# Row maxima of two banks in turn, layer norm's root on ScalarE, named PSUM banks and a new job order

## The chip, the cores and the metric

The kernel runs on one core of a Trainium2 chip. The metric is device time in microseconds (us); lower is better. TensorE (PE in the profile) multiplies and transposes, VectorE (DVE), ScalarE (ACT) and GpSimd (POOL) do the rest, SyncE (SP) issues most transfers.

## The reference

Two branches read the same layer-normed input and are added to it: an infini-attention (segment-wise softmax attention with a compressive memory) and a mixer MLP.

```python
def _A_ref(x, wq, wk, wv, wo, beta):      # S = 2048, D = 512, H = 32 heads of Dh = 16, N = 4 segments of L = 512
    q, k, v = ...                         # x @ wq, x @ wk, x @ wv, split into heads and segments
    phi = lambda t: jnp.where(t > 0, t + 1.0, jnp.exp(t))
    g = _sigmoid(beta).reshape(1, H, 1, 1)
    for s in range(N):
        qs, ks, vs = q[:, :, s], k[:, :, s], v[:, :, s]
        logits = jnp.einsum("bhqd,bhkd->bhqk", qs, ks) * scale + mask      # causal within the segment
        a_dot = jnp.einsum("bhqk,bhkd->bhqd", _softmax(logits), vs)
        pq = phi(qs)
        a_mem = jnp.einsum("bhld,bhde->bhle", pq, M) / (jnp.einsum("bhld,bhd->bhl", pq, z)[..., None] + 1e-6)
        outs.append(g * a_mem + (1.0 - g) * a_dot)
        M = M + jnp.einsum("bhld,bhle->bhde", phi(ks), vs)
        z = z + jnp.einsum("bhld->bhd", phi(ks))
    return ... @ wo
def _B_ref(x, w1, b1, w2, b2):            # F = 1792
    h = _gelu(_layernorm(x) @ w1 + b1)
    return h @ w2 + b2
xn = _layernorm(x)
return x + _A_ref(xn, ...) + _B_ref(xn, ...)
```

## The kernel before

Everything is cut into jobs, and the program is one list of jobs. `ORDER` is a string with one letter a job; each letter names a stream (keys, queries, row maxima, scores, and so on), and the next job of that stream is written out. Each engine runs its own instructions in the order in which the jobs stand in the list, so `ORDER` fixes every engine's queue and the queues of transfers on SP and POOL. The pools around it put in the waits.

The work in words: `X` jobs load four or two tiles of 128 tokens, take their mean and variance (`norm_stats`), scale them (`norm_apply`) and transpose them on TensorE into `xnT`; `Y` does the same for the MLP branch, with statistics that `norm_stats` has made with the first (a norm of a normed row needs only a second root, so `a` and `y` have two columns a tile). `T` projects the queries or keys of 8 heads of one segment (12 matmuls of 512 columns), splits the result into a high and a low half (`hl`) and sends it through DRAM into the layout `qst`/`kst`. There are 16 steps i (4 segments x 4 groups of 8 heads).

In each step the row maxima come first. `m_jobs(i)` makes 12 jobs, for four pairs of heads t and three sets of query blocks: block 3 alone (512 columns of keys), blocks 2 and 0 together (384 + 128), block 1 (256). A job takes two PSUM tiles, one for each head of the pair, multiplies into both, and VectorE then adds the causal mask and takes the maximum, one instruction and one read-out of its result into `mc` for each block. `R` (`m_row`) transposes `mc` on TensorE, halves it (`mhl`, ACT then DVE) and sends it back as two more rows of the queries. `S` jobs compute the scores transposed, with the maximum already taken off, and ScalarE takes the exponential out of PSUM (`pt`); `pv`/`PV` multiply with the values; `O` divides; `Qd`/`Q`/`K`/`Z`/`N` serve the memory (`ame`, `rc`, `mst`, `zr`, `pkn`). `D` is the MLP's first matmul (`hT`), `G` its gelu, `H` the split into halves on POOL and ACT, `e` the second matmul into two tiles that stay open over 14 jobs, and the sum into `acc` (L761) frees them. `out` is the output projection. `warm` jobs are matmuls on ones that keep TensorE busy at the start.

All PSUM tiles come from one pool of 8 (`dense`), each a bank of 128 x 512 numbers. A job that needs a tile waits, on TensorE, until the bank's last reader is done. ScalarE holds one set of function tables at a time: `plan()` puts a load before the first job that needs exponential and logarithm ("E") after a gelu ("G").

Of the kernel before, what the change touches and what calls it, by code (L numbers as in the profile page):

```python
# [57 lines left out]
def streams():  # L58
# [43 lines left out]


ORDER = (
    "aeatcctutcuettcctcvvvatuaatuacevcaaabcvvbccwtvucwvfbtdvbtwvtvxtxxvyxwxxgwxcxyxxhtoooxywocwoosyyniyyzoiyccziigps"
    "iiznipizyinyzcfzAnsiqpiqAizoqqzizAowvpAoimhoAzizjqpjojqqjcczijqibojiBqikkkAAkjiojiqjmjiqjiqjbsqiikkkpkibbaAfopo"
    "jjlgpojlqjjlaohjAokpkkkajojiqijqjAiqijmiqjiqiAsABiBfpoiqqppikkiqiqkkhilBgpoaapolsjqqqjjqqjjoojiiklkkkijpaiaBoos"
    "jqaqjqqiqjiqqiaaBqijqbqqbijqiqsBiifompkkkkibbplmghpooBojqjojljmlqojqqijqikpkkkpiiojiqjqbjqjiqiqijojqiikkkpkliif"
    "nlnigplnrmjjrjjqjniiriqpijqiqikkkkmhjjjrjipiojqiqijpqikikkkbmilolfsoojmjgjolojqjjobbmkkkkmqjiqjqijqjiqjioijoiqi"
    "pisskkkkaphiiqplpqqimislfaolipoqmogaoosmasqqjqjqqjqqjaqjoiiqqiqqppjiqiqooiiipmkkpkkipioijajoqajajqqqqjjiqqsiaho"  # L110
    "akkkkqjslqlbmbjjfojqqljmgjqbbmkkkkmqjqjjohojiiojiojpiikkkkliinoipilmifnilimnigpmrrjjjnrjijrjiikmbpkkkjspiiooisq"
    "ijqjqijqjqbjmipqqiiiqkkkkhilfoqqqpjlmjgojqjqqpjjlmoookkmkkipjipooisqijqiqjjqiqijqqijbbsikkkppkiqqlaiiqmslhfoiqa"
    "qqmppgpoaooojjqaaomojqjjqiqlsqijqqpiqiikkkkmiasiqqjmiqjqqjjpoahojiaqiqjikpkiaoopiaoobfkkpjbjqqjslqlqqqjmjgobbjq"
    "lkmkkkmqjqqjqjqjiqmjqiooijikkkpkpiiiflplonoiliinmiipgniomnrrpjjjoojibqjqijqqiiqpikkkkiqipjrjjqirspjqjisqiqijpqi"
    "kkkkiolfmooljmjgqjbjojqjlmokkkmkjqpojsiiosbqjisqiqijqjqiqijqikkkpkliifbsqqqliiqqmoipgopmloojjojqqjjoojiikkpkkii"
    "qjqijqijqmjpiiqjsqjiqikipikkkpqqioqploplojjqojqjqjqjolkkkkjjqoqjjqpqjsqjoqqkkkkpqqplqpmqpqqqqqqqpqqqqmlqqqqqqlr"
    "rrr"
)


def plan():

    todo = [iter(st) for st in streams()]
    tab = "E"
    for c in "".join(ORDER):
        key = next(todo[NAMES.index(c)])
        k = key[0]
        need = "G" if k == "G" else "E" if k in ("S", "Q") or k == "O" and key[2] == 0 or k == "T" and (
            key[1] >= NG if key[2] == 0 else key[1] < NU - NG) else tab
        yield key, None if need == tab else need  # L130
        tab = need
# [3 lines left out]
def infini_mixer_kernel(ctx: ExitStack, tc: tile.TileContext, x, wq, wk, wv, wo, beta, w1, b1, w2, b2, out):  # L135
    nc = tc.nc
    V, A, G, T, Q = nc.vector, nc.scalar, nc.gpsimd, nc.tensor, nc.sync
# [171 lines left out]
    def qk_scale(g0, n):  # L309
        p = dense()  # L310
        T.matmul(p[:, :2 * n], ones, am[:, :2 * NG].rearrange("p (w g) -> p w g", w=2)[:, :, g0:g0 + n], start=True, stop=True)
# [55 lines left out]
    FV, SV, FO, SO, CO = range(5)  # L367
    F1, S1, F2, S2, CG, SHH, C2, B1F = range(5, 21, 2)

    I_MAGIC = 0x5F3759DF  # L370

    stats = cst.tile([P, S // P, 2, 2], F32, name="stats")

    def norm_stats(tok, tiles):


        n = len(tiles)
        ag = sm.tile([P, 4, 2], F32, name="ag", bufs=1)[:, :n]
# [16 lines left out]
        V.scalar_tensor_tensor(y, b, 1.875, y, op0=OP.add, op1=OP.mult)
# [16 lines left out]
    def ln(kind, n, b, part):  # L412

        tok = 4 * n + 2 * b if kind == "X" else 2 * n
        if part == 0:
            lt[kind, n, b] = ts = []
            for j in range(2):
                name = ("nN", "nD")[j] if (kind, n, b) == ("X", 0, 1) else "xt"
                t = sb.tile([P, D], F32, name=name, bufs=2 if name == "xt" else 1)
                Q.dma_start(t, x[P * (tok + j):P * (tok + j) + P, :])  # L420
                ts.append(t)
        elif part == 1:
            norm_stats(tok, lt[kind, n, b] + (lt[kind, 0, 1] if n == 0 else []))
        else:
            norm_apply(tok, lt[kind, n, b], kind == "Y", (kind, n, b) == ("X", 0, 1))
# [11 lines left out]
    def ln_tr(t, dst, c0):  # L437
        p = dense()
        for k in range(KT):
            T.transpose(p[:, P * k:P * k + P], t[:, P * k:P * k + P], ident)  # L440
# [128 lines left out]
    def m_jobs(i):  # L569
        def f(t, qbs):  # L570
            def go():
                if i not in mc:
                    mc[i] = sm.tile([P, GH, 4], F32, name="mc", bufs=1)
                ps = dense(), dense()
                o = 0
                for qb in qbs:
                    n = P * (qb + 1)
                    for b, p in enumerate(ps):
                        r = slice(64 * b, 64 * b + KM)
                        T.matmul(p[:, o:o + n], stk[i, 0][r, t, P * qb:P * qb + P], stk[i, 1][r, t, :n],  # L580
                                 start=True, stop=True)
                    o += n
                for b, p in enumerate(ps):
                    o = 0
                    for qb in qbs:
                        n = P * (qb + 1)
                        V.tensor_tensor_reduce(p[:, o:o + n], p[:, o:o + n], mask[:, 512 - n:], 1.0, -3e38,  # L587
                                               OP.add, OP.max, mc[i][:, 4 * b + t, qb:qb + 1])
# [249 lines left out]
    for key, load in plan():  # L838
        if load == "E":
            A.preload_act_table_set("natural_log_exp_and_others")  # L840
        CALL[key[0]](*key[1:])
# [28 lines left out]
```

## Time and profile before

| what | us |
|---|---|
| median of 3 runs | 745.69 (745.43 to 746.32) |
| the profiled execution, whole | 747.66 |
| its span, first to last instruction | 745.9 |
| TensorE busy in it | 708.0 |
| VectorE busy | 562.7 |
| ScalarE busy | 536.1 |
| GpSimd busy | 365.3 |
| mean granted TensorE clock | 0.99 of full |

In the profile's rows a group reads: line, engine, operation, output <- inputs, shape, count, then busy time and the mean of one in ns, then the engine's idle time before them and what ended it. A row of waits reads: who waited, for whom, the sum in us, how often, and the longest. A row in order of time reads: start, duration, what. Row maxima appear as CUSTOM_DVE_ANT_0, followed by DVE_READ_ACCUMULATOR2_ANT, the read-out.

### The profile page before, as it was taken

The page shows a single profiled execution, that of the slowest core. Times are in us where ns is not written, and L with a number is a line of the kernel's source. Part 1 is how long each engine was busy: PE and PEld are TensorE (multiplying, and loading weights), DVE is VectorE, ACT ScalarE, POOL GpSimd, SP SyncE. Part 2 cuts the span into 40 slices and gives each one's busy share as a digit, 9 for nine tenths or more (in the row PEclk, how much of TensorE's full clock was granted, in tenths as well). Part 3 has the DMA queues.
Part 4 walks back from the last instruction along what each step waited for, and adds up shares of the span by engine and source line. Part 5 has one row for each costly group of instructions (what it writes and reads, how often), then busy time and mean ns, then how long its engine had stood idle before and what let it go on. Part 6 is the DMA issues. An engine that isn't in the chain of part 4 may idle for free.

```text
span 745.9 us, 16734 instructions
## 1 busy us (share of the span) xinstructions
PE 708.0 (95%) x6261; PEld 397.7 (53%) x6261; DVE 562.7 (75%) x1721; ACT 536.1 (72%) x920; POOL 365.3 (49%) x548
## 2 busy tenths in 40 slices
PE   7899998999999999899999999989999999999997
PEld 5464655464654455455453556565654545564543
DVE  6789878978884877978688677989478575969233
ACT  5788898775986568576884687767685668767960
POOL 5375657465524344535433446455534255355652
PEclk9699999999999999999999999999999999999999
DMA  9765323132304023240412313340311313330001
GB/s 278 217 200 152 105 54 91 45 101 61 100 2 114 29 81 80 58 114 4 108 23 65 102 47 90 79 109 15 88 44 47 112 16 87 86 102 2 3 16 57
DMA packets 54093, 59.30 MB, mean 79 GB/s; under 512 B 5038, under 2 KB 40892, under 8 KB 54012
## 3 DMA queue, kind: packets, MB, share of 16 engines
q1 hardware_dynamic: 51708, 54.04, 25.3%
q0 software_dynamic: 2304, 4.20, 3.5%
q8 instruction: 49, 0.80, 0.5%
q14 instruction: 32, 0.26, 0.1%
HBM read 41.18 MB, written 17.04 MB: 78 GB/s over the span
## 4 chain that ended last, share of the span: by engine, by line
PE 47%; DVE 32%; ACT 7%; issue 5%; POOL 5%; DMA 2%; POOLq 0%; DVEq 0%; SPq 0%; ACTq 0%
PE dense L455 20%; DVE dense L587 13%; PE dense L754 7%; PE dense L649 6%; PE dense L773 4%; PE dense L620 3%; PE dense L580 3%; DVE mc L587 3%; ACT pt L625 2%; DVE hl L475 2%; PE dense L786 1%; PE dense L440 1%; DVE oT L502 1%; DVE zr L517 1%; DVE phk L484 1%
## 5 line engine op out<-in xcount | busy, mean ns | idle before, releaser
L587 DVE CUSTOM_DVE_ANT_0 dense<-dense,mask 128x512 f32<-128x512 f32 (+3 forms) x512 | 240.6, 516 | 25.1 <-PE dense L580 18.2
L625 ACT ACTIVATE pt<-dense,qkcs 128x512 f32<-128x512 f32 (+1 forms) x384 | 207.6, 623 | 43.0 <-PE dense L620 38.1
L754 PE MATMUL dense<-w2s,hT 64*128 64x512 f16 x1344 | 177.3, 376 | 0.6 <-POOL hT L730 0.2
L455 PE MATMUL dense<-yT,w1s 128*128 128x256 f16 x1344 | 160.6, 273 | 6.3 <-DVE mhl L598 1.8
L634 POOL TENSOR_SCALAR_AFFINE_SELECT pt<-pt 128x256 f32<-128x256 f32 x256 | 103.4, 437 | 103.7 <-ACT pt L625 102.4
L455 PEld LDWEIGHTS <-w1s 128*128 128x128 f16 x1344 | 128.2, 98 | 39.2 <-issue 18.8
L730 POOL TENSOR_TENSOR hT<-hh,hT 128x512 f16<-128x512 f32 x64 | 66.7, 1043 | 89.1 <-ACT hT L729 88.6
L754 PEld LDWEIGHTS <-hT 64*128 64x128 f16 x1344 | 71.0, 94 | 62.0 <-issue 12.8
L649 PE MATMUL dense<-pt,vt 128*32 128x512 f32 (+3 forms) x1024 | 77.9, 436 | 0.6 <-POOL pt L634 0.3
L580 PE MATMUL dense<-kst,qst 48*128 48x128 f16 (+3 forms) x512 | 72.3, 297 | 6.4 <-DVE mc L587 2.7
L620 PE MATMUL dense<-qst,kst 50*128 50x512 f16 (+3 forms) x512 | 72.4, 298 | 5.2 <-DVE mc L587 1.6
L587 DVE DVE_READ_ACCUMULATOR2_ANT mc<- 128x1 f32 x512 | 72.1, 141 | 0.2
L729 ACT ACTIVATE hT<-hh 128x512 f16<-128x512 f32 x64 | 36.8, 575 | 29.4 <-POOL hh L728 29.1
L728 POOL TENSOR_SCALAR hh<-hT,sc 128x512 f32<-128x512 f32 x64 | 42.4, 662 | 31.1 <-ACT hT L721 29.0
L649 PEld LDWEIGHTS dense<-pt,vt 128*32 128x32 f32 x1024 | 32.1, 109 | 42.2 <-issue 32.3
L714 ACT ACTIVATE hT<-dense,b1t,sc 128x256 f32<-128x256 f32 x64 | 36.1, 566 | 19.5 <-PE dense L455 18.7
L620 PEld LDWEIGHTS <-kst 50*128 50x128 f16 x512 | 27.3, 94 | 38.7 <-issue 23.8
L580 PEld LDWEIGHTS <-qst 48*128 48x128 f16 x512 | 28.3, 94 | 35.7 <-issue 21.4
L455 PE MATMUL dense<-xnT,wqs 128*128 128x512 f16 x192 | 46.6, 395 | 0.1
L455 PE MATMUL dense<-xnT,wks 128*128 128x512 f16 x192 | 46.6, 395 | 0.1
L679 POOL TENSOR_TENSOR nN<-nN,oT 128x512 f32<-128x512 f32 x16 | 20.3, 1269 | 50.4 <-DVE oT L503 50.4
L475 DVE SCALAR_TENSOR_TENSOR hl<-dense,hl 128x512 f16<-128x512 f32 x32 | 22.1, 690 | 29.9 <-ACT phq L474 11.9
(222 smaller groups left out, 1022.5 us busy)
## 6 DMA issues: line engine op xcount, KB each, us to landing
xt<-in_A_x_dram SPq DMA_DIRECT2D x30, 256.0 KB
kd<-hl SPq DMA_DIRECT2D x48, 128.0 KB
kst<-kd SPq DMA_DIRECT2D x32, 192.0 KB
qd<-hl SPq DMA_DIRECT2D x48, 128.0 KB
qst<-qd SPq DMA_DIRECT2D x32, 192.0 KB
acc<-in_A_x_dram SPq DMA_DIRECT2D x16, 256.0 KB
acc<-in_B_b_dram POOLq DMA_DIRECT2D x16, 256.0 KB, 4.3
out_dram<-acc SPq DMA_DIRECT2D x16, 256.0 KB
```

The source lines that it names most:

```text
L455: T.matmul(p, wsl(ws, k, a), xsl(xs, k, b), start=s0 and i == 0, stop=s1 and i == 3 * n - 1)
L475: V.scalar_tensor_tensor(hl[:, 1, :], p, float(2 ** -16), hl[:, 0, :], op0=OP.mult, op1=OP.subtract)
L580: T.matmul(p[:, o:o + n], stk[i, 0][r, t, P * qb:P * qb + P], stk[i, 1][r, t, :n], start=True, stop=True)
L587: V.tensor_tensor_reduce(p[:, o:o + n], p[:, o:o + n], mask[:, 512 - n:], 1.0, -3e38, OP.add, OP.max, mc[i][:, 4 * b + t, qb:qb + 1])
L620: T.matmul(p[:, o:o + n], stk[i, 1][r, t, P * kb:P * kb + P], stk[i, 0][r, t, P * kb:], start=True, stop=True)
L625: A.activation(e[:, OFF[kbs[0]]:OFF[kbs[0]] + o], p[:, :o], AF.Exp, scale=qkcs[:, 1, i % NG:i % NG + 1])
L634: G.affine_select(v, v, pattern=[[0, 2], [1, P]], compare_op=OP.is_ge, fill=0.0, base=0, channel_multiplier=-1)
L649: T.matmul(p[32 * c:32 * c + 32, P * kb:], vt[s, kb][:, 4 * g + c, 16 * odd:16 * odd + 32], pt[i, 2 * c + odd][:, OFF[kb]:OFF[kb] + LEN[kb ...
L728: G.tensor_scalar(t, hz[:, z, :], col(SHH + j % 2), 0.0, op0=OP.mult, op1=OP.add)
L729: A.activation(hT[:, z, 0, :], t, AF.Copy)
L730: G.tensor_tensor(hT[:, z, 1, :], t, hT[:, z, 0, :], op=OP.subtract)
L754: T.matmul(pes[j][a], hTs[fh][r, fi, u, P * a:P * a + P], w2s[r, fo, v, :], start=n == 0 and m == 0, stop=fi == FH - 1 and m == 2, skip_gr ...
```

## The change

Four things. In `m_jobs` the loops over banks and blocks change places, so that VectorE takes the two banks of a job in turn. In `norm_stats` the reciprocal root, made of an integer shift and polynomial steps on VectorE, becomes exp(-0.5 ln a) on ScalarE with one correcting step on VectorE, and the last two instructions become one; `plan()` therefore asks for the "E" tables for an `X` job's second part. `dense()` takes the bank that the string `BANKS` names, one digit a tile, in place of any free one of 8. `ORDER` is another permutation of the same 1335 jobs.

```diff
-    "aeatcctutcuettcctcvvvatuaatuacevcaaabcvvbccwtvucwvfbtdvbtwvtvxtxxvyxwxxgwxcxyxxhtoooxywocwoosyyniyyzoiyccziigps"
+    "aacttuttcacutvaatcvucuevaatevaacvccvutbcbwtccvtbvvcwfvwtdcvttxxextxvwyxbchxgxxyxoowxoyxowowvyoyzoyzniiibccyygpz"
...
+BANKS = (
+    "012345670123456174052316753401627354106237540612375406123754016237516237516237516231756237153672153675213675213"
...
-        need = "G" if k == "G" else "E" if k in ("S", "Q") or k == "O" and key[2] == 0 or k == "T" and (
+        need = "G" if k == "G" else "E" if k in ("S", "Q") or k == "X" and key[3] == 1 or k == "O" and key[2] == 0 or k == "T" and (
...
+    bank = iter("".join(BANKS))
+
     def dense():
-        return dps.tile([P, 512], F32, name="dense")
+        return dps.tile([P, 512], F32, name="ps" + next(bank), bufs=1)
...
         V.tensor_scalar(a[:, :, 0], ag[:, :, 1], EPS, None, op0=OP.add)
         V.tensor_scalar(a[:, :, 1], ag[:, :, 1], 1.0 + EPS, EPS * EPS, op0=OP.mult, op1=OP.add)
-        V.tensor_scalar(y.bitcast(I32), a.bitcast(I32), 1, None, op0=OP.logical_shift_right)
-        V.tensor_scalar(y.bitcast(I32), y.bitcast(I32), -1, I_MAGIC, op0=OP.mult, op1=OP.add)
-        V.tensor_tensor(b, y, y, op=OP.mult)
-        V.tensor_tensor(b, b, a, op=OP.mult)
+        A.activation(y, a, AF.Ln)
+        A.activation(y, y, AF.Exp, scale=-0.5)
         q = r[:, :, :, 0]
-        V.tensor_scalar(q, b, .375, -1.25, op0=OP.mult, op1=OP.add)
-        V.tensor_tensor(b, b, q, op=OP.mult)
-        V.scalar_tensor_tensor(y, b, 1.875, y, op0=OP.add, op1=OP.mult)
         V.tensor_tensor(b, y, y, op=OP.mult)
         V.scalar_tensor_tensor(b, b, -0.5, a, op0=OP.mult, op1=OP.mult)
         V.scalar_tensor_tensor(q, b, 1.5, y, op0=OP.add, op1=OP.mult)
-        for j in range(2):
-            V.scalar_tensor_tensor(r[:, :, j, 1], ag[:, :, 0], -1.0, r[:, :, j, 0], op0=OP.mult, op1=OP.mult)
+        V.scalar_tensor_tensor(r[:, :, :, 1], ag[:, :, 0:1].broadcast_to([P, n, 2]), -1.0, q, op0=OP.mult, op1=OP.mult)
...
-                for b, p in enumerate(ps):
-                    o = 0
-                    for qb in qbs:
-                        n = P * (qb + 1)
+                o = 0
+                for qb in qbs:
+                    n = P * (qb + 1)
+                    for b, p in enumerate(ps):
                         V.tensor_tensor_reduce(p[:, o:o + n], p[:, o:o + n], mask[:, 512 - n:], 1.0, -3e38,
                                                OP.add, OP.max, mc[i][:, 4 * b + t, qb:qb + 1])
-                        o += n
+                    o += n
```

Lines of the changed kernel stand ten further down from the norm on (L587 becomes L597, L598 becomes L608, L714 becomes L724, and so on); the norm's first lines, L386 and L387, become L402 and L403.

What stands in a row on an engine changes at three places. Names carry their buffer's number; `dense` becomes `ps` with the bank's digit; what an instruction waits for stands in brackets, by engine or transfer queue.

The first place: VectorE, the first job of blocks 2 and 0 in the program. An ISA row with an input is a maximum, one without is its read-out. Before:

```order
L587 ISA dense_697,mc_670<-dense_697,mask_81 128x384 [waits PE_49]
L587 ISA mc_670 128x1
L587 ISA dense_697,mc_670<-dense_697,mask_81 128x128 [waits DVE_49]
L587 ISA mc_670 128x1
L587 ISA dense_698,mc_670<-dense_698,mask_81 128x384 [waits PE_49]
L587 ISA mc_670 128x1
L587 ISA dense_698,mc_670<-dense_698,mask_81 128x128 [waits DVE_49]
L587 ISA mc_670 128x1
```

And now:

```order
L597 ISA ps2_690,mc_683<-ps2_690,mask_81 128x384 [waits PE_49]
L597 ISA mc_683 128x1
L597 ISA ps3_691,mc_683<-ps3_691,mask_81 128x384 [waits PE_49]
L597 ISA mc_683 128x1
L597 ISA ps2_690,mc_683<-ps2_690,mask_81 128x128 [waits DVE_49]
L597 ISA mc_683 128x1
L597 ISA ps3_691,mc_683<-ps3_691,mask_81 128x128 [waits DVE_49]
L597 ISA mc_683 128x1
```

The narrow maximum, which waits for VectorE's own write to the same bank, moves from right behind that write to one maximum later.

The second place: VectorE, the end of the norm of the third segment's first two tiles, with the row maxima of step 6 (`mhl`) beside it. Before:

```order
L394 TENSOR_TENSOR nw_4312<-nw_4312,stats_109 128x4 [waits DVE_49]
L395 SCALAR_TENSOR_TENSOR nw_4312<-nw_4312 128x4 [waits DVE_49]
L396 TENSOR_TENSOR nw_4312<-nw_4312 128x4 [waits DVE_49]
L397 SCALAR_TENSOR_TENSOR nw_4312<-nw_4312 128x4 [waits DVE_49]
L398 SCALAR_TENSOR_TENSOR stats_109<-nw_4312 128x4 [waits DVE_49]
L400 SCALAR_TENSOR_TENSOR stats_109<-ag_4305,stats_109 128x2 [waits DVE_49]
L400 SCALAR_TENSOR_TENSOR stats_109<-ag_4305,stats_109 128x2
L598 SCALAR_TENSOR_TENSOR mhl_4345<-dense_4343,mhl_4345 32x128 [waits Activation_49]
L716 TENSOR_SCALAR hT0_112<-dense_4355,sc_106,b1t_114 128x256 [waits PE_49]
L761 SCALAR_TENSOR_TENSOR acc_3768<-dense_3627,sc_106,acc_3768 128x512 [waits DMASW4_49,PE_49]
```

And now:

```order
L608 SCALAR_TENSOR_TENSOR mhl_4301<-ps7_4299,mhl_4301 32x128 [waits Activation_49]
L771 SCALAR_TENSOR_TENSOR acc_3431<-ps4_3831,sc_106,acc_3431 128x512 [waits DMASW4_49,PE_49]
L771 SCALAR_TENSOR_TENSOR acc_3981<-ps1_3832,sc_106,acc_3981 128x512 [waits DMASW5_49]
L397 BN_STATS st_4328<-xt_4209 128x6 [waits DMAHW2_49]
L398 BN_AGGR ag_4327<-st_4328 128x2 [waits DVE_49]
L397 BN_STATS st_4331<-xt_4211 128x6 [waits DMAHW3_49]
L398 BN_AGGR ag_4327<-st_4331 128x2 [waits DVE_49]
L402 TENSOR_SCALAR nw_4334<-ag_4327 128x2 [waits DVE_49]
L403 TENSOR_SCALAR nw_4334<-ag_4327 128x2
L407 TENSOR_TENSOR nw_4334<-nw_4334 128x4 [waits Activation_49]
L408 SCALAR_TENSOR_TENSOR nw_4334<-nw_4334 128x4 [waits DVE_49]
L409 SCALAR_TENSOR_TENSOR stats_109<-nw_4334 128x4 [waits DVE_49]
```

`mhl` and the sums into `acc` move ahead of the norm, and the norm itself is shorter, with a wait for ScalarE (Activation) in its middle.

The third place: ScalarE, at the norm of the same segment's other two tiles. Before, exponentials of the scores and then `mhl`:

```order
L625 ACTIVATE pt_4893<-dense_4925,qkcs_108 128x512 [waits PE_49]
L625 ACTIVATE pt_4894<-dense_4926,qkcs_108 128x512 [waits PE_49]
L625 ACTIVATE pt_4893<-dense_4935,qkcs_108 128x256 [waits PE_49]
L625 ACTIVATE pt_4894<-dense_4936,qkcs_108 128x256 [waits PE_49]
L597 ACTIVATE mhl_4966<-dense_4964 32x128 [waits DMAHW0_49,PE_49]
```

And now:

```order
L635 ACTIVATE pt_4839<-ps5_4869,qkcs_108 128x512 [waits PE_49]
L635 ACTIVATE pt_4840<-ps4_4870,qkcs_108 128x512 [waits PE_49]
L635 ACTIVATE pt_4839<-ps6_4887,qkcs_108 128x256 [waits PE_49]
L635 ACTIVATE pt_4840<-ps1_4888,qkcs_108 128x256 [waits PE_49]
L404 ACTIVATE nw_4902<-nw_4902 128x4 [waits DVE_49]
L405 ACTIVATE nw_4902<-nw_4902 128x4 [waits Activation_49]
L724 ACTIVATE hT1_113<-ps3_4920,b1t_114,sc_106 128x256 [waits PE_49]
L607 ACTIVATE mhl_4936<-ps0_4934 32x128 [waits DMAHW1_49,PE_49]
```

The two activations of the root (L404 and L405) come behind the exponentials and ahead of an evacuation of the MLP (L724) and `mhl`. The program has 33 table loads before and now.

More of the change, by code (lines that the diff above doesn't have):

```diff
@@ L104 @@
 ORDER = (
-    "aeatcctutcuettcctcvvvatuaatuacevcaaabcvvbccwtvucwvfbtdvbtwvtvxtxxvyxwxxgwxcxyxxhtoooxywocwoosyyniyyzoiyccziigps"
[L106 to L114, printed above, removed]
@@ L115 @@
-    "kkkkiolfmooljmjgqjbjojqjlmokkkmkjqpojsiiosbqjisqiqijqjqiqijqikkkpkliifbsqqqliiqqmoipgopmloojjojqqjjoojiikkpkkii"
-    "qjqijqijqmjpiiqjsqjiqikipikkkpqqioqploplojjqojqjqjqjolkkkkjjqoqjjqpqjsqjoqqkkkkpqqplqpmqpqqqqqqqpqqqqmlqqqqqqlr"
-    "rrr"
+    "aacttuttcacutvaatcvucuevaatevaacvccvutbcbwtccvtbvvcwfvwtdcvttxxextxvwyxbchxgxxyxoowxoyxowowvyoyzoyzniiibccyygpz"
+    "iiccniipznzyiyfzAnsqpiioiqizzmAqqiwpAzhoAoiiqqzzjpocjiqijjqizjoAjoBAiikskkAkjqiqjqmjjisqjiojiqbiskkkpkibbplafoA"
+    "oAjpgjloojqjqjqjlohakkkpkojiqiAajsoijijqjiqjmiAiAifippBkkqqBikipqikoqilBsgaoplahqjjqlqqqjqjoBoijqiajqipamkkkksa"
@@ new lines @@
+    "ioojpiqjqiqijqjiaaqjqjsbmqiqBiiBfoikkkbBpkbibpghopoolqqpjqojjjloojiqjqiqilmkpkkkijojiqqqijjqijqiqjqiipkkkpkbiif"
+    "mnillnglnnrjjrjqiirpjiqjisqijqikkmkkjijrjjioijioijikkpkkhilmfolomjjbgojqqjpljqjoobsmbkkkkjqqisjqqjijqiqjiqijoiq"
+    "iiskkmippqiqpiskaklmiohlfoiqpqaqamqgploooaomjqjqqjqmjqaojpqpsiiqiqoioiqjpqiqiikkkkoapjiqijqijqjpqiqjqsjaqaoihkk"
+    "kkaalmoqjjlbfobqjqjlsqmjgbbqjkkmmkkjqjqmojjjohiojiikkkkipiifplilonnliiiniipmripgnojjmjrjsjorijibkkkpkmiiqjqjqij"
+    "qqiijsqiqjohjqiiqpqiipmkpkkskrillfmmlogqqbjjoojqjqjjoomkkpkkiijhooiqjiqjqijqiqpsjiqqjibbpqiqipkkkkliiqaslfoioom"
@@ new lines @@
+    "papqqqamgpooasjqqjqjmaoojqjlqjqiqiapqikmkikkiqipoiqjqjaoohijqjaqiqiisopaojiqqjiakmspkkklbopfjqlbqjmjgqjjqqjqlob"
+    "bkkkmkmjqjqqiqjqijqjqoimijkpkkkliilfnimiiplgnniipirmoiorponijpjobojjioisjqqjpiiqkkkkiiprijsqsqjiqqjjimqqijrijkk"
+    "ipkbsklfloqjqmjglojjqqqjjomsokkkkopjmioiijojqijqipqjqjqiiqqiikppkkkliqlfbbqliqqqimoipmgooojpjqqjojjoomjiikkkpki"
+    "qijqijqjqiijqjiqjqiikisqpiskkkqpioqplooplqjjqqjjojjqlopkkkkjqjqqjjojqjoqqpspqkkkkqpqqlqqpqqmpqqqqqqqqqqqmqllqqr"
+    "rrr"
+)
+BANKS = (
+    "012345670123456174052316753401627354106237540612375406123754016237516237516237516231756237153672153675213675213"
+    "675213765726132567132567132561723516725314607314607314067430167340176340167430167430164301643701643016743021543"
+    "021435140235143021542301540123540125340125340152340152403156274031562740351640351640531640513645013465016354016"
+    "354016354016354016534016534160543154602731452670315426073154206734215063741253741065370265237065237062537056237"
+    "052635270635270652706523706532741534271354274135271435271435271435217406357214035610431054613054613054613054630"
+    "546135045061345067123450673152046731520467315204637152046371520463715204637120543670512437065172065210765027106"
+    "257106257106257106275062701652704136572043162045731625371627513627153627153627153627513267521376503476547036543"
+    "706543765403765403765437403765403765403746052416052461052104621054621056421056241602543176032154760321547603215"
+    "746032157460321576403215764302157642157641572647215762415274627154761245671267456741253607412536401720513674203"
+    "764230764230764230764230764203726403752614037512640735124065214502615401256405126405164052164052164051264703512"
+    "64351263451263470"
@@ L368, in infini_mixer_kernel @@
     F1, S1, F2, S2, CG, SHH, C2, B1F = range(5, 21, 2)
-    I_MAGIC = 0x5F3759DF
     stats = cst.tile([P, S // P, 2, 2], F32, name="stats")
```

## Prediction

> **What bounds the kernel now.** I read the page first: the busy shares, then the chain that ended last, by engine and by line.
>
> ```profile
> span 745.9 us, 16734 instructions
> PE 708.0 (95%) x6261; PEld 397.7 (53%) x6261; DVE 562.7 (75%) x1721; ACT 536.1 (72%) x920; POOL 365.3 (49%) x548
> PE 47%; DVE 32%; ACT 7%; issue 5%; POOL 5%; DMA 2%; POOLq 0%; DVEq 0%; SPq 0%; ACTq 0%
> PE dense L455 20%; DVE dense L587 13%; PE dense L754 7%; PE dense L649 6%; PE dense L773 4%; PE dense L620 3%; PE dense L580 3%; DVE mc L587 3%; ACT pt L625 2%; DVE hl L475 2%; PE dense L786 1%; PE dense L440 1%; DVE oT L502 1%; DVE zr L517 1%; DVE phk L484 1%
> ```
>
> TensorE looks busy 95% of the time, yet less than half of the chain is its own: 32% is VectorE, and L587, the row maxima with their read-outs, holds 13 + 3 = 16%, 119 us. Second, the view by stages (PE, PEld, DVE, ACT, POOL busy in us):
>
> ```profile
> 0.00:50.00 50.00, 42.23 (x261) 29.50 (x261) 34.81 (x108) 36.25 (x66) 26.88 (x40) 0.86 0.76 220
> 50.00:700.00 650.00, 625.51 (x5678) 349.96 (x5678) 514.02 (x1593) 479.33 (x821) 318.73 (x482) 1.00 0.27 72
> 700.00:746.00 46.00, 40.21 (x325) 18.21 (x324) 13.82 (x21) 20.52 (x34) 19.69 (x28) 0.99 0.10 30
> 200.00:250.00 50.00, 50.00 (x410) 25.07 (x411) 36.50 (x115) 32.48 (x56) 20.17 (x33) 1.00 0.21 57
> 300.00:350.00 50.00, 44.51 (x424) 26.17 (x420) 43.27 (x145) 32.01 (x54) 23.56 (x33) 1.00 0.26 65
> ```
>
> From 50 to 700 us PE idles 650 - 625.5 = 24.5 us. It idles most (5.5 us) where DVE is busiest (43.3 of 50) and not at all where DVE has 36.5. So VectorE's queue decides PE's holes. The recorded idle is also not all that PE loses, as two rows by shape and in order of time show:
>
> ```profile
> L580 PE MATMUL dense<-kst,qst 48*128 48x512 f16 x128 | 29.8, 378 | 2.6 <-DVE hT L716 1.4 <-DVE mc L587 0.5 <-DVE mst L564 0.2
> 300.83 2.75 PE L455 MATMUL dense<-xnT,wks 128*128 128x512 f16 x12
> ```
>
> A 512-column matmul in a stream takes 2.75 / 12 = 0.23 us. The 128 score matmuls of that width are 64 pairs on two halves of the array: at 0.23 each that is 15 us, while they are recorded busy for 29.8. Short waits are hidden in such lone matmuls' own latency. Third, who PE waited for:
>
> ```profile
> PE dense L595 <- DVE mc L587: 4.3, 6, 1.5
> PE dense L311 <- ACT wqs L295: 3.3, 1, 3.3
> PE dense L580 <- DVE mc L587: 2.7, 7, 0.5
> PE dense L455 <- DVE mhl L598: 1.8, 1, 1.8
> PE dense L580 <- DVE hT L716: 1.8, 3, 0.8
> PE dense L620 <- DVE mc L587: 1.6, 4, 0.7
> PE dense L455 <- DVE ame L534: 1.2, 1, 1.2
> PE dense L620 <- DVE hT L716: 1.1, 2, 0.9
> ```
>
> All but one of these are VectorE. The kernel alternates between PE and DVE as the bound.
>
> **Row maxima in turn.** The timeline of DVE, start and duration, around one job with two blocks per bank, and the end of the last such job:
>
> ```profile
> 299.61 0.47 DVE L587 CUSTOM_DVE_ANT_0 dense<-dense,mask 128x256 f32<-128x256 f32 x1
> 299.99 0.14 DVE L587 DVE_READ_ACCUMULATOR2_ANT mc<- 128x1 f32 x1
> 299.99 0.73 DVE L587 CUSTOM_DVE_ANT_0 dense<-dense,mask 128x512 f32<-128x512 f32 x1
> 300.64 0.14 DVE L587 DVE_READ_ACCUMULATOR2_ANT mc<- 128x1 f32 x1
> ...
> 301.98 0.56 DVE L587 CUSTOM_DVE_ANT_0 dense<-dense,mask 128x384 f32<-128x384 f32 x1
> 302.46 0.14 DVE L587 DVE_READ_ACCUMULATOR2_ANT mc<- 128x1 f32 x1
> 302.63 0.30 DVE L587 CUSTOM_DVE_ANT_0 dense<-dense,mask 128x128 f32<-128x128 f32 x1
> 302.85 0.14 DVE L587 DVE_READ_ACCUMULATOR2_ANT mc<- 128x1 f32 x1
> 302.85 0.60 DVE L587 CUSTOM_DVE_ANT_0 dense<-dense,mask 128x384 f32<-128x384 f32 x1
> 303.36 0.14 DVE L587 DVE_READ_ACCUMULATOR2_ANT mc<- 128x1 f32 x1
> 303.54 0.30 DVE L587 CUSTOM_DVE_ANT_0 dense<-dense,mask 128x128 f32<-128x128 f32 x1
> 303.76 0.14 DVE L587 DVE_READ_ACCUMULATOR2_ANT mc<- 128x1 f32 x1
> ...
> 686.85 0.14 DVE L587 DVE_READ_ACCUMULATOR2_ANT mc<- 128x1 f32 x1
> 687.03 0.30 DVE L587 CUSTOM_DVE_ANT_0 dense<-dense,mask 128x128 f32<-128x128 f32 x1
> ```
>
> When the next maximum is in the other bank, it starts with the read-out, on top of it (299.99 and 299.99, 302.85 and 302.85). When it is in the same bank (384, then 128), it starts 0.17 to 0.18 us later (302.46 to 302.63, 303.36 to 303.54, 686.85 to 687.03): the program gives it a wait on the engine's own earlier write. There are 128 of these, as the count of the 128-wide shape says:
>
> ```profile
> L587 DVE CUSTOM_DVE_ANT_0 dense<-dense,mask 128x128 f32<-128x128 f32 x128 | 38.3, 300 | 4.4
> ```
>
> In turn, the waiting one comes two places later and its predecessor's write is long done. DVE gains 128 x 0.175 = 22.4 us. How much lies on the path: per step the four shapes take, start to start, 0.65 + 0.69 + 0.22 + 0.38 = 1.94 us a bank, so 64 (16 steps of 4 pairs of heads) x 2 x 1.94 = 248 us in all, of which the chain holds 119, or 48%. I take 0.48 x 22.4 = 10.8 us. Ends: a gain of all 22.4; a loss, since the first bank is released one maximum later (0.52 + 0.52 + 0.22 = 1.26 us after the job's start, not 0.69 + 0.22 = 0.91) while the second comes free 0.35 us sooner. If PE always waited for the first bank alone, 64 x 0.35 x 0.48 = 10.8 us would be lost. PE takes banks in pairs, so the second decides and I stay with the gain.
>
> A rule of the Trainium skill speaks against this. "VectorE: DVE Perf Modes", section "The DRAIN you can't avoid", says that every VectorE operation is followed by a flush and that a semaphore between two of them "costs nothing extra here". By it the term would be 0 and the sum 738.7. The rows disagree: with the wait 0.17 to 0.18 us, without it 0.00.
>
> **Layer norm's root.** Seven calls. From L386 to the second L400 a call is 14 small VectorE instructions; the six calls after the start, each in its own window of the stage view, give together
>
> ```profile
> sum 22.66, DVE 20.38; mean DVE 3.40
> 488.01 1.16 POOL L730 TENSOR_TENSOR hT<-hh,hT 128x512 f16<-128x512 f32 x1 [0.75 <-ACT hT L729]
> 488.11 1.07 DVE L395 SCALAR_TENSOR_TENSOR nw<-nw 128x4 f32<-128x4 f32 x1
> L597 ACT ACTIVATE mhl<-dense 32x128 f16<-32x128 f32 x16 | 4.1, 259 | 5.4 <-PE dense L595 5.2
> ```
>
> 22.66 us, some of it a tiny operation that stands 1.07 us beside a GpSimd one. Six of 14 instructions stay: 6/14 x 22.66 = 9.7 us. In their middle DVE now waits for two dependent activations on ScalarE; the nearest small one takes 0.26 us, and with a handoff each way I take 0.6 us a call, 3.6 us. DVE gains 22.7 - 9.7 - 3.6 = 9.4 us. What waits behind these blocks today is the work after them on DVE's queue, as the second place above shows for mhl: the waits of 1.8 (mhl), 1.8 and 1.1 (hT), 1.2 (ame) are 5.9 us. Not all stand behind a norm, so I take 4. Ends: a gain of 9.4; a loss with the wait on ScalarE, priced as a rival. Queued behind Ln on ACT is the next evacuation (the third place: L724, then mhl's), behind L407 on DVE the next row maxima or acc. ScalarE itself gets 14 x 0.26 = 3.6 us more work beside 210 us of idle; I cost it at nothing, and 3.6 us if it has no slack there. The first call lies ahead of the first transposes, but PE's wait there (3.3 us) is for the weights' squares on ACT: nothing, at most 1.5 us (9.4 / 6) if that cover is gone. Table loads stay 33 in number; one more pair would cost 2 x 1.28 us:
>
> ```profile
> L840 ACT ACT_TABLE_LOAD x16 | 20.5, 1283 | 0.3
> L625 ACT ACTIVATE pt<-dense,qkcs 128x512 f32<-128x512 f32 x256 | 159.2, 693 | 30.0 <-PE dense L620 29.6
> ```
>
> **Order and banks.** No instruction or DMA is added; jobs move past each other on all five queues, SP's and POOL's too, and the next bank is named instead of taken from what is free. The trace of before can't price it. Downward end: what is left of the recorded idle after the two terms, 24.5 - 14.8 = 9.7 us. Upward: of the thirteen 50 us stages from 50 to 700, the mean one idles 24.5 / 13 = 1.9 us and the one from 300 is 3.6 us worse; three more like it would cost 11 us. At the second place mhl moves ahead of the norm, which is worth the 1.8 us wait by itself; I take a gain of 3, near the better end only in that.
>
> **Sum.** -10.8 - 4 - 3 = -17.8 us. The profiled execution took 747.66 us, 1.76 around its span; the median of the runs is 745.69, 2 us lower. I take the difference from the median: 745.69 - 17.8 = 727.9, so 728. The start and the end of the program (idle 7.8 and 5.8 us) I leave as they are.
>
> **Rivals.**
> - The root's round trip costs more than it saves: slower. In the order, Ln stands behind four exponentials of up to 0.69 us in three of the six later calls (the third place is one), which wait for PE, and DVE stands still meanwhile, with PE's banks behind it. At a wait of w a call the norm's term is 6w + 9.7 - 22.7, in place of -4. The change turns slower when 6w exceeds 13 + 10.8 + 3, at w = 4.5 us; at 5.5 us it gives 745.7 - 13.8 + 20 = 752. For it: ACT is 72% busy and in order. Against: the wait for a group is at most 4 x 0.69 = 2.8 us unless PE is late.
> - TensorE is the bound after all and VectorE's gain falls into its idle time: 745.7, no change. For it: 95% busy, and the stage from 200 with no hole. Against: 32% DVE on the chain.
> - The gap between maxima is not from the shared bank but follows each wide maximum, whatever comes next, and stays: the other two terms alone, -7, 738.7. Against it: the 0.00 rows. The page named above would have it so.
> - DVE's gains all reach the path and the order closes the rest: 745.7 - 22.4 - 5.9 - 9.7 = 707.7. For it: the waits hidden in short matmuls, more than the recorded idle.
>
> **How the numbers follow.** Forecast 0.62 (its own range 715 to 740), round trip 0.10, no change 0.07, gap stays 0.08, everything reaches the path 0.13. A measurement of this kernel can't tell less than 0.2%, 1.5 us, from no change. Faster: 0.62 + 0.08 + 0.13 = 0.83; same 0.07; slower 0.10. The range leaves out the slower rival and the lower half of the last: 710 to 745, which takes in the bounds of the first term (738.7 at zero) and of the order (+11 from the forecast, 742).
>
> **What would show it.** Right: the 128-wide maximum starts with the read-out before it; a norm block of six VectorE instructions near 2.2 us; 33 table loads; the L587 line's successor under 15% of the chain; PE's waits for mc, mhl and hT shrunk. Wrong: idle of DVE before L407 of several us a call, released by ACT; or DVE less busy, PE's idle from 50 to 700 still near 24 us, and new waits on ACT's pt or on a bank in their place.

## The result and the profile after

The changed kernel takes 713.25 us (median; 712.69 to 714.16) against 746.01 for the kernel before beside it, a ratio of 0.9558 (95% interval 0.9537 to 0.9579): 33 us gained where 18 were forecast. The profiled execution's span is 711.0 us. From its page, the span, the busy shares, and the chain by engine and by line:

```profile
span 711.0 us, 16718 instructions
PE 693.3 (98%) x6261; PEld 392.6 (55%) x6261; DVE 531.8 (75%) x1665; ACT 535.9 (75%) x934; POOL 363.7 (51%) x548
PE 67%; DVE 12%; ACT 8%; DMA 6%; POOL 4%; issue 3%; SPq 1%; POOLq 0%; DVEq 0%; ACTq 0%
PE ps L465 26%; PE ps L764 14%; PE ps L659 8%; PE ps L783 6%; PE ps L630 4%; PE ps L590 4%; DVE ps L597 4%; ACT pt L635 3%; DMA kd<-hl 2%; PE ps L450 2%; PE ps L538 1%; DVE hl L485 1%; DMA w1s<-in_B_w_dram 1%; DVE mc L597 1%; DMA pt<-in_A_wv_dram 1%
```

VectorE's part of the chain went from 32% to 12%, and that of the row maxima from 16% to 4 + 1 = 5%. VectorE is busy for 562.7 - 531.8 = 31 us less; the chain is TensorE's now. The stages (columns as before: PE, PEld, DVE, ACT, POOL busy):

```profile
0.00:50.00 50.00, 41.58 (x287) 29.38 (x288) 37.11 (x104) 40.06 (x76) 29.77 (x42) 0.97 0.89 252
50.00:667.00 617.00, 613.08 (x5662) 345.62 (x5664) 480.78 (x1541) 476.85 (x830) 315.90 (x484) 1.00 0.28 73
667.00:711.00 44.00, 38.61 (x317) 17.59 (x309) 13.92 (x21) 18.98 (x30) 18.05 (x24) 1.00 0.10 31
300.00:350.00 50.00, 49.94 (x492) 30.10 (x492) 36.62 (x113) 41.54 (x76) 27.93 (x44) 1.00 0.26 68
```

The middle stage has nearly the same matmuls (5662 here, 5678 before) in 617 us rather than 650. Of these 33 us, TensorE's recorded idle gives 24.5 - 3.9 = 20.6, and its recorded busy time 625.5 - 613.1 = 12.4. Some 1.7 of the 12.4 are the 16 matmuls fewer, at 613.1 / 5662 us each. So about a third of the gain lay in time that the profile had called busy. 6.9 of the 12.4 are in the score matmuls; two rows of the page before and the same two after:

```profile
L580 PE MATMUL dense<-kst,qst 48*128 48x128 f16 (+3 forms) x512 | 72.3, 297 | 6.4 <-DVE mc L587 2.7
L620 PE MATMUL dense<-qst,kst 50*128 50x512 f16 (+3 forms) x512 | 72.4, 298 | 5.2 <-DVE mc L587 1.6
```

```profile
L630 PE MATMUL ps<-qst,kst 50*128 50x512 f16 (+3 forms) x512 | 70.6, 298 | 0.1
L590 PE MATMUL ps<-kst,qst 48*128 48x512 f16 (+3 forms) x512 | 67.2, 298 | 0.7 <-DVE hT L726 0.4
```

One matmul takes as long as before (297 or 298 ns); the groups' times, in which matmuls that overlap count once, are 6.9 us shorter, and the idle time ahead of them fell from 11.6 to 0.8 us. What TensorE still waits for stands mostly at the start, above all in the preparation of the weights on ScalarE (the longest of its waits):

```profile
PE ps L329 <- ACT wqs L313: 2.0, 1, 2.0
PE ps L346 <- ACT wvs L313: 2.0, 1, 2.0
PE ps L796 <- POOL ones L174: 1.6, 1, 1.6
PE ps L346 <- ACT w1s L313: 1.5, 1, 1.5
PE ps L465 <- DVE phk L495: 1.2, 1, 1.2
PE ps L450 <- POOL xt L418: 0.7, 1, 0.7
PE ps L465 <- DVE mc L597: 0.6, 2, 0.4
```

VectorE's timeline at a job with two blocks a bank (start, duration): each maximum now starts with the read-out before it.

```profile
55.23 0.59 DVE L597 CUSTOM_DVE_ANT_0 ps<-ps,mask 128x384 f32<-128x384 f32 x1
55.75 0.14 DVE L597 DVE_READ_ACCUMULATOR2_ANT mc<- 128x1 f32 x1
55.75 0.59 DVE L597 CUSTOM_DVE_ANT_0 ps<-ps,mask 128x384 f32<-128x384 f32 x1
56.26 0.14 DVE L597 DVE_READ_ACCUMULATOR2_ANT mc<- 128x1 f32 x1
56.26 0.33 DVE L597 CUSTOM_DVE_ANT_0 ps<-ps,mask 128x128 f32<-128x128 f32 x1
56.51 0.14 DVE L597 DVE_READ_ACCUMULATOR2_ANT mc<- 128x1 f32 x1
56.51 0.33 DVE L597 CUSTOM_DVE_ANT_0 ps<-ps,mask 128x128 f32<-128x128 f32 x1
```

### The profile page after: what moved, and what is told of

It is laid out like the page before. It is cut to its first block, busy times and chain, and to the rows that moved or that the text cites. A ratio compares the mean times of both kernels' runs of the same rounds, so it can differ in the third digit from the quotient of the medians.

```text
span 711.0 us, 16718 instructions
## 1 busy us (share of the span) xinstructions
PE 693.3 (98%) x6261; PEld 392.6 (55%) x6261; DVE 531.8 (75%) x1665; ACT 535.9 (75%) x934; POOL 363.7 (51%) x548
## 4 chain that ended last, share of the span: by engine, by line
PE 67%; DVE 12%; ACT 8%; DMA 6%; POOL 4%; issue 3%; SPq 1%; POOLq 0%; DVEq 0%; ACTq 0%
PE ps L465 26%; PE ps L764 14%; PE ps L659 8%; PE ps L783 6%; PE ps L630 4%; PE ps L590 4%; DVE ps L597 4%; ACT pt L635 3%; DMA kd<-hl 2%; PE ps L450 2%; PE ps L538 1%; DVE hl L485 1%; DMA w1s<-in_B_w_dram 1%; DVE mc L597 1%; DMA pt<-in_A_wv_dram 1%
## 5 line engine op out<-in xcount | busy, mean ns | idle before, releaser
L597 DVE CUSTOM_DVE_ANT_0 ps<-ps,mask 128x512 f32<-128x512 f32 (+3 forms) x512 | 235.0, 524 | 24.1 <-PE ps L590 23.2
L635 ACT ACTIVATE pt<-ps,qkcs 128x512 f32<-128x512 f32 (+1 forms) x384 | 206.9, 628 | 20.2 <-PE ps L630 17.7
L764 PE MATMUL ps<-w2s,hT 64*128 64x512 f16 x1344 | 176.2, 376 | 0.3 <-DVE fence L767 0.2
L465 PE MATMUL ps<-yT,w1s 128*128 128x256 f16 x1344 | 161.2, 273 | 2.5 <-DVE phk L495 1.2
L659 PE MATMUL ps<-pt,vt 128*32 128x512 f32 (+3 forms) x1024 | 77.6, 436 | 0.1
L597 DVE DVE_READ_ACCUMULATOR2_ANT mc<- 128x1 f32 x512 | 72.6, 142 | 0.2
L630 PE MATMUL ps<-qst,kst 50*128 50x512 f16 (+3 forms) x512 | 70.6, 298 | 0.1
L590 PE MATMUL ps<-kst,qst 48*128 48x512 f16 (+3 forms) x512 | 67.2, 298 | 0.7 <-DVE hT L726 0.4
L724 ACT ACTIVATE hT<-ps,b1t,sc 128x256 f32<-128x256 f32 x64 | 36.6, 571 | 17.1 <-PE ps L465 16.6
L465 PE MATMUL ps<-xnT,wqs 128*128 128x512 f16 x192 | 45.0, 384 | 0.4 <-DVE mc L597 0.4
L783 PE MATMUL ps<-wos,oT 128*128 128x512 f16 x192 | 44.0, 380 | 0.9 <-POOL oT L695 0.6
L465 PE MATMUL ps<-xnT,wks 128*128 128x512 f16 x192 | 44.2, 380 | 0.0
L726 DVE TENSOR_SCALAR hT<-ps,sc,b1t 128x256 f32<-128x256 f32 x48 | 25.7, 539 | 24.5 <-PE ps L465 24.4
L590 PEld LDWEIGHTS <-qst 48*128 48x128 f16 x512 | 27.1, 94 | 30.7 <-issue 14.8
```

What stands on the lines that cost most here:

```text
L465: T.matmul(p, wsl(ws, k, a), xsl(xs, k, b), start=s0 and i == 0, stop=s1 and i == 3 * n - 1)
L630: T.matmul(p[:, o:o + n], stk[i, 1][r, t, P * kb:P * kb + P], stk[i, 0][r, t, P * kb:], start=True, stop=True)
L635: A.activation(e[:, OFF[kbs[0]]:OFF[kbs[0]] + o], p[:, :o], AF.Exp, scale=qkcs[:, 1, i % NG:i % NG + 1])
L659: T.matmul(p[32 * c:32 * c + 32, P * kb:], vt[s, kb][:, 4 * g + c, 16 * odd:16 * odd + 32], pt[i, 2 * c + odd][:, OFF[kb]:OFF[kb] + LEN[kb ...
L764: T.matmul(pes[j][a], hTs[fh][r, fi, u, P * a:P * a + P], w2s[r, fo, v, :], start=n == 0 and m == 0, stop=fi == FH - 1 and m == 2, skip_gr ...
L783: T.matmul(p, o[:, u, P * b:P * b + P], wos[:, g, v, :], start=i == 0, stop=i == 3 * NG - 1)
```

## The experiments

Two theories stood after the result. One: the new order lets VectorE's freed time reach TensorE, and the two edits of VectorE's work are the gain. The other: the order closes TensorE's holes by itself, and the edits add what was forecast or less. Differences below are between medians, each against the kernel before in the same comparison (746.0 to 746.8 us).

### Both of VectorE's edits, old order, one pool

The old `ORDER` and `dense` pool with both edits of `m_jobs` and `norm_stats`.

> Old job order and pool, with both VectorE edits (maxima in turn, root on ScalarE). If VectorE's freed time is what the change is worth, this takes about two thirds of the 33 us: 720 to 728. If the new order is what counts and the old one is fitted to the slower VectorE, it takes a third or less: 735 to 740.

739.05 us, -7.5 (ratio 0.9901, 0.9873 to 0.9930).

### New order and named banks, VectorE's work as before

The complement: the `+` lines of `ORDER`, `BANKS` and `dense`, and none of the others.

> New job order and named banks, with VectorE's work as before. If VectorE's freed time is what counts: 735 to 742, or slower than before since the order is fitted to shorter maxima. If the order is what counts: 718 to 728.

725.22 us, -21.4 (0.9716, 0.9695 to 0.9737). So the order with its banks carries about two thirds of the change by itself, and the first theory falls. Its middle stage:

```profile
50.00:680.00 630.00, 619.46 (x5658) 343.04 (x5660) 501.54 (x1589) 474.79 (x818) 314.97 (x483) 1.00 0.27 72
300.00:350.00 50.00, 49.34 (x479) 30.22 (x477) 41.05 (x138) 35.97 (x63) 25.32 (x40) 1.00 0.23 63
```

Of the 20 us less than before, 24.5 - 10.5 = 14.0 are recorded idle time and 6 recorded busy time. The stage from 300 us has hardly a hole (0.7 us), with VectorE busy for 41 of 50. The two halves add up to -28.9, the whole is -32.8: some 4 us come only when both are there, little more than the three intervals together leave open (about 3 us).

### The order without the names, and the whole without the names

```diff
-        return dps.tile([P, 512], F32, name="ps" + next(bank), bufs=1)
+        return dps.tile([P, 512], F32, name="dense")
```

> New job order alone, banks from the pool, VectorE's work as before. If naming the banks matters, this is several us slower than the same with named banks; if the pool picks as well, within 1.5 us of it.

> The changed kernel with banks from the pool in place of the named ones. If naming is worth nothing: 712 to 715. If the names are fitted to the predicted release times and carry part of the gain: 718 to 725.

The order alone: 728.13 us, -18.5 (0.9749, 0.9724 to 0.9773). The changed kernel with the pool: 715.47 us, -31.1 (0.9589, 0.9566 to 0.9612). Naming the banks is worth 2 to 3 us in either pair, at the edge of what the intervals can tell, and less than the several us that were expected of names that matter; the order is worth the rest.

### Each of VectorE's edits alone

The diff's hunk of `m_jobs` alone, then that of `norm_stats` alone (with its word in `plan`), in the old order.

> The kernel before with only the row maxima of two banks in turn. With the layer norm's edit beside it the old order came to 739.1 us, 7.5 us under its before. Theory M (the gain is VectorE's freed time, and the maxima free 18.4 us against the norm's 10.4): 739 to 741.5, so 5 us or more of the 7.5. Rival N (the gain is the norm's shorter wait for mhl and hT): 742 to 745. If the new order alone carries most of the change, both stay far above 725.

> The kernel before with only the layer norm's root on ScalarE. Theory M: 743 to 746, since only six blocks a run are shortened. Rival N: 739 to 742. Slower than before (747 or more) if the round trips to ScalarE cost more than the eight VectorE operations that they replace.

Maxima in turn: 739.27 us, -7.5 (0.9902, 0.9880 to 0.9924), all that both edits gave. The root alone: 747.86, +1.0 (1.0012, 0.9999 to 1.0025): no change that can be told, where 743 to 746 was expected. Its blocks became shorter as planned, from 22.66 to 11.49 us for the six later calls. What took over shows in the stage view of one call and the sum over the six, and in two of TensorE's waits (the first was 0.8 us before, the second not in the list):

```profile
311.00:312.50 1.50, 0.32 (x2) 0.19 (x2) 0.85 (x6) 1.24 (x4) 0.00 (x0) 1.00 0.71 196
sum 11.49, PE 9.94 PEld 5.60 DVE 6.89 ACT 9.16 POOL 3.24; mean PE 1.66 PEld 0.93 DVE 1.15 ACT 1.53 POOL 0.54
PE dense L612 <- DVE phq L477: 2.4, 1, 2.4
PE dense L447 <- ACT hT L706: 1.3, 1, 1.3
```

TensorE still stands during that call, the one behind which it had waited 1.8 us for `mhl`. Now it waits 1.3 us for ScalarE's evacuation of `hT`. ScalarE's row says why. Two rows of the kernel before, and what stands there with the root on ScalarE:

```profile
304.30 0.68 ACT L474 ACTIVATE phk<-dense,qksc 128x512 f32<-128x512 f32 x1
304.93 0.56 ACT L714 ACTIVATE hT<-dense,b1t,sc 128x256 f32<-128x256 f32 x1
```

```profile
303.63 0.68 ACT L466 ACTIVATE phk<-dense,qksc 128x512 f32<-128x512 f32 x1
311.23 0.21 ACT L386 ACTIVATE nw<-nw 128x4 f32<-128x4 f32 x1 [6.92 <-DVE nw L385]
311.47 0.21 ACT L387 ACTIVATE nw<-nw 128x4 f32<-128x4 f32 x1
311.58 0.55 ACT L706 ACTIVATE hT<-dense,b1t,sc 128x256 f32<-128x256 f32 x1
```

Ln now stands ahead of `hT` in ScalarE's row, and ScalarE sits idle for 6.92 us until VectorE has the variance; the evacuation of `hT`, which was done by 305.5, starts at 311.58. At the call of 485 us it is the same: ScalarE waits 4.76 us at Ln, the evacuation of `rc` behind it starts at 486.04 where it started at 483.13, and the wait for `phq` is the one that grew to 2.4. In all, Ln waits for VectorE for 16.8 us, in five of seven calls; in the changed kernel it is 5.3 us in three, and neither wait of TensorE is in its list. At the start ScalarE delays the first call: Ln comes at 11.95 us, behind the squares of the weights, and TensorE waits 3.2 us for the first normed tiles, a wait that the kernel before hardly had (its wait for `wqs` there fell from 3.3 to 2.1 us).

```profile
11.32 0.63 ACT L295 ACTIVATE wks<-pt 128x512 bf16<-128x512 f32 x1 [0.16 <-DMA pt<-in_A_wk_dram]
11.95 0.19 ACT L386 ACTIVATE nw<-nw 128x8 f32<-128x8 f32 x1
PE dense L432 <- POOL xt L400: 3.2, 1, 3.2
```

### The changed kernel less one edit

The same two hunks undone in the changed kernel, one at a time.

> The changed kernel with the row maxima one bank after the other again. New order and named banks alone gave 725.2 us, all together 713.3: 12 us lie on the two VectorE edits. Theory M: 721 to 724 (8 to 11 us lost). Rival N: 715 to 719. If the two edits only pay together, because VectorE must be quick at both for the new order, this and the kernel without the root lose 8 us or more each.

> The changed kernel with the layer norm's root on VectorE again. Theory M: 715 to 718 (2 to 5 us lost). Rival N: 720 to 724. If the two edits only pay together: 721 or more, and the kernel without the turn as well.

Without the turn: 720.89 us, -25.9 (0.9653, 0.9628 to 0.9677). Without the root: 716.35 us, -30.5 (0.9598, 0.9580 to 0.9616). So in the new order the turn gives 6.9 us on top of the root and 9.1 without it, and the root 2.3 on top of the turn (3.0 by the ratios) and 4.5 without it. The two do not need each other; the root needs the new order.

### Where in the program the order earns its time

Old pool and old VectorE work; the first 224 of 1335 jobs in the one order, the remaining ones in the other.

> The kernel before (its pool and VectorE's work as they were) whose first 224 jobs, up to about 80 us of TensorE's work, stand in the new order; all later ones in the old. The new order alone gave 18.5 us. Theory S (spread): the gain is gathered all along, about a third of it in this stretch: 738 to 742. Theory P (one place): the gain lies at the start, and this kernel has nearly all of it: 727 to 732; or it lies behind it, and this one is at 745 to 748.

> The other half: the first 224 jobs in the old order, all later ones in the new, pool and VectorE's work as before. Theory S: 732 to 737. Theory P: 727 to 730 where the gain lies behind the start, 744 to 747 where it lies at the start.

The new start alone: 743.28 us, -3.0 (0.9968, 0.9957 to 0.9979). The new order behind an old start: 731.99 us, -14.3 (0.9811, 0.9789 to 0.9832). The sum is close to the order alone (-18.5). The gain is gathered mostly behind the start: the first run was expected at 738 to 742 if the gain were gathered all along, a third of it in this stretch, and has less. The stage from 300 us, of the new start and then of the old:

```profile
300.00:350.00 50.00, 44.20 (x430) 26.80 (x431) 41.66 (x136) 31.54 (x56) 25.44 (x38) 1.00 0.27 65
300.00:350.00 50.00, 49.50 (x479) 31.09 (x479) 43.12 (x145) 34.11 (x60) 24.52 (x37) 1.00 0.23 58
```

The hole of 5.8 us is there under the old order and gone (0.5) under the new, with VectorE busier in the second.

### Half of VectorE's row maxima, in both orders

```diff
-                        V.tensor_tensor_reduce(p[:, o:o + n], p[:, o:o + n], mask[:, 512 - n:], 1.0, -3e38,
+                        V.tensor_tensor_reduce(p[:, o:o + n // 2], p[:, o:o + n // 2], mask[:, 512 - n:512 - n // 2], 1.0, -3e38,
```

> The kernel before, whose row maxima take only the first half of each bank's columns (part of the maximum is left out): 1280 columns x 2 banks x 64 halved, about 80 us of VectorE's time less, with all else as it was. Theory V (the old order loses its time to moments in which VectorE is behind): 712 to 726. Rival W (it loses it elsewhere, to ScalarE, GpSimd and the transfers): 732 to 742.

> New order and named banks with VectorE's work as before, row maxima over half the columns (part of the maximum is left out). Theory V: the order earns its time by spreading VectorE's work, so with VectorE relieved the two orders come closer: 705 to 715, at most 12 us under the old order with the same halved maxima. Rival W: the order's 21 us stay whole, so 18 us or more under it.

Old order: 725.89 us, -20.4 (0.9731, 0.9700 to 0.9761); new order: 710.70, -35.5 (0.9531, 0.9516 to 0.9546). The first lies at the upper end of what was set for theory V (712 to 726, the old order loses its time to moments in which VectorE is behind), not where the rival has it (732 to 742). The second test came out between the theories: the order is still worth 15.2 us when VectorE does 75 us less, against 21.4 with its full work, where V allows 12 and the rival asks for 18. The old order's executions run from 722.75 to 727.96 us, so that the 15.2 is good to some 2.5. Neither theory holds whole: some 6 of the 21 us go with VectorE's load, the larger part does not. The old order with halved maxima shows two of the places, in the stage from 300 us and its longest waits:

```profile
300.00:350.00 50.00, 44.98 (x442) 25.79 (x440) 34.21 (x129) 32.49 (x57) 20.96 (x35) 0.97 0.29 72
PE dense L455 <- DVE mhl L598: 2.2, 1, 2.2
PE dense L455 <- ACT pt L625: 2.2, 1, 2.2
```

VectorE is busy for only 34.2 of 50 us here, and TensorE idles 5.0 us all the same. What the two waits end with stands in VectorE's row and in ScalarE's:

```profile
301.35 0.67 DVE L386 TENSOR_SCALAR nw<-ag 128x2 f32<-128x2 f32 x1
...
304.70 0.23 DVE L400 SCALAR_TENSOR_TENSOR stats<-ag,stats 128x2 f32<-128x2 f32 x2
304.85 0.27 DVE L598 SCALAR_TENSOR_TENSOR mhl<-dense,mhl 32x128 f16<-32x128 f32 x1
```

```profile
322.17 0.63 ACT L729 ACTIVATE hT<-hh 128x512 f16<-128x512 f32 x1 [1.19 <-POOL hh L728]
322.81 1.28 ACT L840 ACT_TABLE_LOAD   x1
324.11 0.84 ACT L625 ACTIVATE pt<-dense,qkcs 128x256 f32<-128x256 f32 x2
```

`mhl` is ready for VectorE (its first half left ScalarE at 300.9) and stands behind the norm's 3.5 us; `pt` stands behind the end of a gelu and a table load. Halving the maxima shortens neither. In the new order alone (old VectorE work, pool) `mhl` runs at 302.28 and the norm's block begins at 305.51, and neither wait is in the list of that stage. So the first hole is VectorE's queue after all, by what stands ahead of what and not by how busy it is.

## Why the prediction was right or wrong

The direction was right, and so was the mechanism of the maxima. The time, 713, lies in the range but 2 us outside the forecast's own band (715 to 740): in the part that the range took from the rival in which all of VectorE's gains reach the path and the order closes the rest. The first half of that did not come true and the second brought more than was put on it, so that it is luck that the time lies in the range; each of VectorE's terms was put too high and the order's far too low. Term by term:

- **Row maxima in turn, -10.8: measured -7.5 in the old order, -6.9 to -9.1 in the new.** The wait on the same bank is gone, 0.00 where it was 0.17 to 0.18, so the rival "the gap stays" (738.7) falls, and with it the rule of the Trainium skill ("VectorE: DVE Perf Modes", section "The DRAIN you can't avoid") as the prediction applied it. The prediction left out that the same section says "A next op that is not held starts earlier" (the page calls held what starts only when every earlier operation has finished); the 0.00 rows agree with that. The freed time was smaller than 22.4 us: the narrow maximum now takes 0.25 us to its read-out (56.26 to 56.51), not 0.22, which takes back 128 x 0.032 = 4 us. What of the remaining 18.4 us reached the end is 7.5 / 18.4 = 41%, beside the 48% that the chain's share gave. The rival in which all of VectorE's gains reach the path is refuted: halving the maxima took 562.7 - 488.0 = 74.7 us from VectorE and gave 20.4, or 27%.
- **Layer norm's root, -4: measured +1.0 in the old order, -2.3 to -4.5 in the new.** VectorE's freed time was well estimated: 22.66 to 12.32 us for the six blocks, against 9.4 forecast. So was the round trip in the new order: the first row below is the sum over the changed kernel's six blocks, and the second gives the wait for ScalarE as 5.5 us for seven calls, 0.8 a call beside 0.6, far from the 4.5 at which the slower rival begins.

```profile
sum 12.32, PE 12.32 PEld 8.73 DVE 7.18 ACT 9.48 POOL 5.49; mean PE 2.05 PEld 1.46 DVE 1.20 ACT 1.58 POOL 0.91
L407 DVE TENSOR_TENSOR nw<-nw 128x4 f32<-128x4 f32 (+1 forms) x7 | 1.6, 230 | 5.5 <-ACT nw L405 5.5
```

  The step that failed in the old order is "what waits behind these blocks". The prediction asked how long VectorE would wait for ScalarE and not how long ScalarE would stand at Ln until VectorE had the variance: 16.8 us in five calls, with the evacuations of `hT` and `rc` behind it, so that TensorE waited for those in place of `mhl` and `ame`. Of the 5.9 us of waits that the term was taken from, the order with its banks left 1.2 us, all for `hT`; most of them were the order's to remove.
- **Order and banks, -3: measured -21.4 alone.** This is the term that was mis-sized, and with it the whole difference. Its downward end was "what is left of the recorded idle after the two terms, 9.7 us". That bound contradicts the prediction's own reading that the recorded idle isn't all that TensorE loses: in the end 12.4 of 33 us came out of recorded busy time. How much that is the reading had not shown: the 128 widest score matmuls, 29.8 us where it counted 15, still take 28.1 in the changed kernel, so that 1.7 of these 14.8 us came back. The bound also took the two other terms' full value off the idle first, as if each of their microseconds closed a hole; the edits alone closed far less. The Trainium skill warns of that measure: "Perfetto Trace Analysis", section "Identifying the Most-Contended Engine", calls TensorE's busy share a poor measure of how close a kernel is to its roofline, because pipelined instructions look smaller in the trace. The trace agrees that the share misleads, since the recorded busy time of the same 6261 matmuls fell from 708.0 to 693.3 us; here matmuls looked larger, not smaller, where waits stood between them (the two groups of score matmuls above).
- **"VectorE's queue decides PE's holes".** It was read from two stages, the one with most holes being the one with VectorE busiest. As a matter of VectorE's load this did not hold: the hole of 5.5 us stayed at 5.0 with VectorE at 34.2 us in place of 43.3, and went when the order alone changed. As a matter of what stands ahead in its queue it held for `mhl`, behind the norm; the other wait there, `pt`, is ScalarE's. The list behind "all but one of these are VectorE" leaves out three waits as long as those in it: `w1s` (2.6) and `pt` (1.4) on ScalarE, `ones` (1.6) on GpSimd. The forecast priced the 1.8 us for `mhl` by itself; the stage had 5.5 - 0.7 = 4.8 us in it for the order and its banks.
- **Start and end "as they are".** The end is (46 to 44 us with the same idle time, 5.8 and 5.4). The new order's start gave 3.0 us, some of it perhaps the clock's (last section).
- **ScalarE's added work at nothing, 33 table loads.** The loads are 33, and in the new order nothing speaks against the rest. In the old one it was not the work that cost but its place in ScalarE's row, at the two calls above and at the start, where the prediction had put at most 1.5 us and TensorE waited 3.2 for the first tiles.

What is still open: which of the order's moves, beside those in the stage from 300 us, make up the 15 us that do not depend on VectorE's load. For the root in the old order the two calls and the start show what took its gain, but they were not added up to its whole time. Moves one at a time were not tried.

## What to carry to other kernels

Price a new order by the lost time in each stage, not by the idle time in TensorE's record: count the matmuls of a stage and compare what they take in a stage without holes. Before a hole is put down to the engine that is busy beside it, look at what the waiting matmul waits for and what stands ahead of that in its engine's queue; if it is other work, such as a norm or a table load, a move in the order helps where shorter work elsewhere doesn't. And when work goes to another engine, ask what will stand behind it there while it waits for its input. Here a microsecond taken off the second engine's longest work was worth a quarter to a half of one at the end, and 11 us taken off the norm's blocks were worth nothing while Ln held ScalarE's row.

## What the runs showed of the hardware

A maximum over 128 columns takes 0.22 us to its read-out when it follows its own bank's wide maximum after a wait, and 0.25 us when it follows another bank's without one, so that 0.14 of the 0.175 us of waiting was gained. The granted clock of the first 50 us differs from profile to profile: the kernel with the new start and the one with the old, first in each row the stage, third from the end the clock:

```profile
0.00:50.00 50.00, 41.19 (x286) 29.68 (x287) 36.65 (x112) 39.51 (x72) 29.26 (x42) 0.97 0.92 256
0.00:50.00 50.00, 42.70 (x265) 29.70 (x266) 35.92 (x108) 36.54 (x67) 27.49 (x41) 0.86 0.80 229
```

That the order of jobs makes this difference is not shown. Profiles of one execution each read 0.93 to 1.00 for kernels with the new start and 0.86 to 0.93 for those with the old, but executions of one kernel differ as much: the mean clock of the kernel before, over whole executions, went from 0.990 to 0.998 in the comparison with these two, and 0.998 leaves no more than 0.002 x 746 = 1.5 us of clock to lose, so by estimate some 0.97 or more over the first 50 us. Its four executions at 0.998 took 744.3 to 745.4 us and the one at 0.990 took 747.6, so that, by estimate, up to some 3 us between two executions can be the clock's. How much of the start's 3.0 us is the clock's was not tried.
